# A streaming attention decode kernel: seven instead of five output blocks behind the last V quarter, the last transfer in two pieces, three more fillers, and one gather matmul per pair of heads

## The chip, the cores and the metric

One NeuronCore of one Trainium2 chip. The metric is the device time of one execution in microseconds (us). Executions are repeated, each kernel in the same rounds on the same chip as the kernel before. Two terms recur: a transfer has landed when the trace shows it finished, and the granted clock is the share of TensorE's full clock that the trace shows (1.00 is full, 0.50 half).

## The reference, cut to what matters

Four residual layers, numbered 0 to 3 here, weights A, B, A, B, one query token:

```python
# per layer: x = x + attention(layernorm(x)) @ wo
q = layernorm(x) @ wq                       # D = 640 -> 32 heads x 192
scores = einsum("bhqd,bhkd->bhqk", q, k_cache) * 192 ** -0.5   # 8192 keys a head
p = softmax(scores)
o = einsum("bhqk,bhkd->bhqd", p, v_cache)
x = x + o.reshape(1, 1, 6144) @ wo
```

All inputs are bfloat16. Every layer reads its K and V caches (about 100 MB each) once, which, with the weights, is where the 849 MB of an execution come from; a little of the first two layers is kept on the chip for the last two.

## The kernel before

Heads go in 16 pairs per layer. K and V stream into eight slots of SBUF. VectorE (DVE) multiplies K by q, TensorE (PE) sums the products with an identity matrix, softmax follows, and PE multiplies by V. A pair then has its sums on four groups of 32 partitions (a "gather" adds them up), and after every fifth pair the row of heads is turned into columns and multiplied by a block of wo.

The gather of a pair, with one FP32 matmul per head, both to PSUM partition 96:

```python
def gather(p):
    end = p == NPAIR - 1
    a, n = (slice(0, P), 1) if end else (slice(96, 97), 2)
    ...                                      # DVE: acc = sum of 8 groups of columns
    PE.wait(e, last["TO"], last["TT"])
    for h in range(2):
        if end:
            ...                              # the last pair goes to columns directly
        else:
            e = PE.op(lambda t, h=h: t.matmul(
                TB[96:97, C_O + h * DH:C_O + (h + 1) * DH], lhsT=half[:, h:h + 1], rhs=acc[:],
                start=True, stop=True), signal=h == 1, bank=TBu)
```

The order of the last transfers of layers 1 and 3, with NB wo blocks ("wob") kept back behind the last V quarter ("vq"), and the last pair's three blocks of wo ("wol") at the very end. "wol" is issued only when the columns of the first 15 pairs have been made:

```python
NB = [0, 5, 0, 5]
plan.insert(-2, ("wo", l, 2))                # 15 - NB blocks, ahead of the last pair's V
...
plan.append(("vq", l))                       # last quarter of the last pair's V
both(("wob", l))                             # NB blocks
both(("wol", l))                             # 3 blocks of the last pair
```

Filler matmuls, whose result nobody reads, stand where PE would be idle near the end: `busy(16)` ahead of the gather of pair 14, and in layer 3 `busy(6)` ahead of the wait for the last V quarter:

```python
def busy(n):
    PE.wait(ev_const, last["S"][0])
    for i in range(n):                       # identity x identity, 512 columns, to a free bank
        ...
```

## Time and profile before

| | before |
|---|---|
| median of the first three runs | 1982.81 us (1982.56 to 1983.79) |
| the same with three more runs | 1983.24 us (1982.22 to 1986.6) |
| span of the profiled run | 1980.6 us |
| DMA queue, share of 16 engines | 99.6% |
| from the landing of the last V quarter to the end | 6.4 us |

The page's lines on the busy shares, the stream and the chain stand in the prediction. To these belong the groups that the gather touches, and PE's first summing matmul of each K, L609 (line, engine, operation, out<-in, shapes, count | busy us, mean ns | idle before, releaser):

```profile
L705 PE MATMUL TB<-acc,small 128*1 128x192 f32 x240 | 81.8, 491 | 212.0 <-DVE acc L694 212.0
L716 ACT ACTIVATE rows<-TB,small 1x192 bf16<-1x192 f32 x120 | 43.2, 405 | 590.6 <-PE TB L705 590.6
L609 PE MATMUL S<-pool,ident 128*128 128x512 bf16 x128 | 62.3, 487 | 203.9 <-DVE pool L596 203.8
```

Read the first line so: 60 pairs, two heads, two records each, are 240; PE is busy with them for 81.8 us, and before them it sat idle for 212 us waiting for DVE. It is the idle time that says how little the 81.8 us are worth. In the timeline of the kernel before, one ordinary pair (start, duration, what, idle time before):

```profile
1921.64 1.44 PE L705 MATMUL TB<-acc,small 128*1 128x192 f32 x4 [3.68 <-DVE acc L694]
1923.12 0.72 ACT L716 ACTIVATE rows<-TB,small 1x192 bf16<-1x192 f32 x2 [8.01 <-PE TB L705]
1926.61 6.77 DVE L596 TENSOR_TENSOR pool<-pool,q_sb 128x3072 bf16<-128x3072 bf16 x4 [5.02 <-DMA pool<-in_B_k_cache_dram]
...
1928.43 0.61 PE L609 MATMUL S<-pool,ident 128*128 128x512 bf16 x1 [5.34 <-DVE pool L596]
```

After the gather PE is idle for another 5.34 us, until DVE has multiplied the next K; and DVE itself had waited 5.02 us for that K to land.

### The profile page before, as it was taken

What the parts mean: (1) busy time and instruction counts of PE and PEld (TensorE: products, weight loads), DVE (VectorE), ACT (ScalarE), POOL (GpSimd) and SP (SyncE); (2) the same over time, 40 slices, a digit from 0 to 9 for tenths busy, and PEclk for the clock granted to TensorE, in tenths of its full rate; (3) what the DMA queues carried; (4) which work ended last, traced back from release to release, by engine and by line L of the source; (5) the groups of instructions that cost most, each with busy time, mean ns of one, the idle gap of its engine ahead of it and who ended that gap; (6) DMA issues with size and microseconds to landing.
All of it is one profiled execution on the core that took longest, in us unless ns stands there. A gap on an engine that the chain in (4) does not pass through costs nothing.

```text
span 1980.6 us, 13743 instructions
## 1 busy us (share of the span) xinstructions
PE 1288.7 (65%) x8245; PEld 146.4 (7%) x3159; DVE 1201.3 (61%) x1376; ACT 139.9 (7%) x462; POOL 4.5 (0%) x23
## 2 busy tenths in 40 slices
PE   3567476666466666665785675666676766666658
PEld 0001001000200100100020010010002001001001
DVE  3567467467166656566745565665764775665756
ACT  0000000000000000000010000000000100000000
POOL 0000000000000000000000000000000000000000
PEclk9787776778587777777787778877886878777779
DMA  9999999999999999999999999999999999999998
GB/s 413 435 435 429 430 430 433 436 428 429 436 430 431 430 435 433 427 433 432 426 412 431 426 429 432 431 428 432 431 430 428 435 431 435 431 432 432 431 432 367
DMA packets 26786, 849.25 MB, mean 429 GB/s; under 512 B 3042, under 2 KB 3044, under 8 KB 3812
## 3 DMA queue, kind: packets, MB, share of 16 engines
q1 hardware_dynamic: 26580, 848.38, 99.6%
q8 instruction: 45, 0.74, 0.2%
q14 instruction: 17, 0.14, 0.0%
q10 hardware_dynamic: 144, 0.00, 0.0%
HBM read 848.36 MB, written 0.00 MB: 428 GB/s over the span
## 4 chain that ended last, share of the span: by engine, by line
DMA 67%; PE 19%; DVE 12%; ACT 1%; issue 0%; SPq 0%
DMA pool<-in_B_k_cache_dram 27%; DMA pool<-in_A_v_cache_dram 22%; DMA pool<-in_A_k_cache_dram 13%; DVE pool L596 10%; PE S L58 10%; DMA pool<-in_B_v_cache_dram 6%; PE OY L58 5%; PE OY L675 3%; DVE acc L694 1%; ACT p_sb L633 1%; DVE s_sb L618 1%; PE S L609 1%; PE OY L535 0%; DVE m_bf L620 0%; PE QM L623 0%
## 5 line engine op out<-in xcount | busy, mean ns | idle before, releaser
L596 DVE TENSOR_TENSOR pool<-pool,q_sb 128x3072 bf16<-128x3072 bf16 x512 | 861.1, 1753 | 235.0 <-DMA pool<-in_B_k_cache_dram 139.5
L58 PE MATMUL S<-pool,ident 128*128 128x512 bf16 x2944 | 793.4, 428 | 17.0 <-DVE pool L596 15.4
L705 PE MATMUL TB<-acc,small 128*1 128x192 f32 x240 | 81.8, 491 | 212.0 <-DVE acc L694 212.0
L58 PE MATMUL OY<-pool,p_sb 128*16 128x512 bf16 x1920 | 198.1, 488 | 0.0
L693 DVE TENSOR_SCALAR acc<-OY,small 128x192 f32<-128x192 f32 x64 | 26.7, 418 | 281.1 <-PE OY L58 251.6
L609 PE MATMUL S<-pool,ident 128*128 128x512 bf16 x128 | 62.3, 487 | 203.9 <-DVE pool L596 203.8
L675 PE MATMUL OY<-pool,p_sb 128*16 128x512 bf16 (+1 forms) x1216 | 146.3, 489 | 67.4 <-DMA pool<-in_A_v_cache_dram 59.9
L694 DVE SCALAR_TENSOR_TENSOR acc<-OY,small,acc 128x192 f32<-128x192 f32 x424 | 177.1, 418 | 14.9
L618 DVE TENSOR_REDUCE s_sb<-S 128x64 f32<-128x512 f32 x128 | 88.0, 688 | 68.0 <-PE S L58 68.0
L524 ACT ACTIVATE q_sb<-QM 128x192 bf16<-128x192 f32 x60 | 19.9, 331 | 949.8 <-PE QM L518 949.8
L716 ACT ACTIVATE rows<-TB,small 1x192 bf16<-1x192 f32 x120 | 43.2, 405 | 590.6 <-PE TB L705 590.6
L689 DVE RECIPROCAL small<-TB 1x2 f32<-1x2 f32 x64 | 11.2, 175 | 94.9 <-PE TB L648 75.2
L633 ACT ACTIVATE p_sb<-s_sb,small 64x128 bf16<-64x128 f32 x128 | 55.7, 435 | 160.8 <-DVE small L627 160.0
L609 PEld LDWEIGHTS S<-pool,ident 128*128 128x128 bf16 x128 | 12.9, 101 | 683.1 <-DVE pool L596 589.1
L648 PE MATMUL TB<-small,ones 128*1 128x2 f32 x120 | 11.4, 165 | 74.1 <-ACT p_sb L633 74.1
L675 PEld LDWEIGHTS OY<-pool,p_sb 128*16 128x16 bf16 (+1 forms) x1216 | 38.9, 106 | 213.4 <-issue 137.2
L623 PE MATMUL QM<-ident,m_bf 128*64 128x64 bf16 x128 | 14.1, 217 | 54.4 <-DVE m_bf L620 53.8
L705 PEld LDWEIGHTS TB<-acc,small 128*1 128x1 f32 x240 | 19.7, 101 | 308.1 <-DVE acc L694 280.7
L627 DVE TENSOR_REDUCE small<-QM 128x1 f32<-128x64 f32 x64 | 14.4, 225 | 35.2 <-PE QM L623 35.2
L518 PEld LDWEIGHTS QM<-rows,one_b 1*64 1x64 bf16 x120 | 6.2, 100 | 344.2 <-issue 338.4
L535 PE MATMUL OY<-oT,pool 128*128 128x1 bf16 x675 | 28.6, 178 | 1.9 <-ACT oT L581 1.9
L535 PEld LDWEIGHTS OY<-oT,pool 128*128 128x128 bf16 x675 | 27.8, 131 | 3.8 <-ACT oT L581 2.5
(74 smaller groups left out, 218.3 us busy)
## 6 DMA issues: line engine op xcount, KB each, us to landing
pool<-in_B_k_cache_dram SPq DMA_DIRECT2D x28, 6144.0 KB, 38.3
pool<-in_B_v_cache_dram SPq DMA_DIRECT2D x28, 6144.0 KB, 34.5
pool<-in_A_v_cache_dram SPq DMA_DIRECT2D x27, 6144.0 KB, 27.6
pool<-in_A_k_cache_dram SPq DMA_DIRECT2D x34, 3072.0 KB, 20.3
pool<-in_A_k_cache_dram SPq DMA_DIRECT2D x14, 6144.0 KB, 36.4
pool<-in_A_v_cache_dram SPq DMA_DIRECT2D x10, 3072.0 KB, 14.2
pool<-in_B_k_cache_dram SPq DMA_DIRECT2D x8, 3072.0 KB, 22.6
pool<-in_A_wo_dram SPq DMA_DIRECT2D x6, 2400.0 KB, 21.8
```

Of the source, the lines that this page charges most:

```text
L58: return t.add_instruction(mybir.InstMatmult(name=t.bass.get_next_instruction_name(), engine=mybir.EngineType.PE, ins=[t.lower_ap(rhs), t. ...
L524: lambda a: a.activation(q_sb[i][:], QM[:, 0:DH], ACT.Copy), e, last["q"][i], bank=QMu)
L535: e = PE.op(lambda t, i=i, c=c, f=y_first[0], fin=n[0] == "wol" and i == k - 1: t.matmul(YB[:, c:c + 1], lhsT=t3[:, i, c:D:DC], rhs=o[:, i ...
L596: e = DV.op(lambda v, d0=d0: v.tensor_tensor(k3[:, :, d0:d0 + QD], kin[:, :, d0:d0 + QD], q_sb[qi][:, d0:d0 + QD].unsqueeze(1).broadcast_t ...
L609: t.matmul(S[:, :], lhsT=ident[:], rhs=k3[:, :, d0:d0 + R], start=True, stop=fin) if d0 == 0 else
L618: lambda v, u=u: v.tensor_reduce(s[:, u * JU:(u + 1) * JU], SP_[u][:].rearrange("p (j r) -> p j r", r=R), AX.X, ALU.add), ev_S[p, u], last ...
L633: ev_p[p] = AC.op(lambda a, h=h, r=r: a.activation(p_sb[par][r, :, h], s[r, :], ACT.Exp, bias=negm[par][r, 0:1], accum_out=l_col[par][r, h ...
L675: t.matmul(o, lhsT=x, rhs=y, start=f, stop=fin) if c == 0 else
L693: v.tensor_scalar(acc[:], O[:, 0:DH], pick[:, 0:1], None, ALU.mult) if i == 0 else
L694: v.scalar_tensor_tensor(out=acc[:], in0=O[:, i * DH:(i + 1) * DH], scalar=pick[:, i:i + 1], in1=acc[:], op0=ALU.mult, op1=ALU.add)), e if ...
L705: e = PE.op(lambda t, h=h: t.matmul(TB[96:97, C_O + h * DH:C_O + (h + 1) * DH], lhsT=half[:, h:h + 1], rhs=acc[:], start=True, stop=True), ...
L716: last["TO"] = last["row_written"] = AC.op(lambda a, h=h: a.activation(orow[:, o0 + h * DH:o0 + (h + 1) * DH], TB[96:97, C_O + h * DH:C_O ...
```

## The change

Its intent: shorten what stands behind the last V quarter in layer 3, and spend less of PE on the gather. Cut to its core:

```diff
-    NB = [0, 5, 0, 5]
+    NB = [0, 5, 0, 7]
+        both_h = sb("both_h", [P, 33], F32)          # column 0: head 0, column 32: head 1, zero between
             both(("wol", l))
+            if l == 3:
+                both(("woe", l))                     # wol: two blocks, woe: the third, own semaphore
...
-                        e = PE.op(lambda t: t.matmul(TB[96:97, C_L:C_L + 2], lhsT=ones[:, 0:1], rhs=l_col[par][:],
+                        e = PE.op(lambda t: t.matmul(TB[64:97, C_L:C_L + 2], lhsT=ones[:, 0:1].broadcast_to([P, 33]), rhs=l_col[par][:],
...
+                if end and l == 3:
+                    busy(3)
                 PE.wait(e, last["TO"], last["TT"])
-                for h in range(2):
+                for h in range(2 if end else 1):
...
-                        e = PE.op(lambda t, h=h: t.matmul(
-                            TB[96:97, C_O + h * DH:C_O + (h + 1) * DH], lhsT=half[:, h:h + 1], rhs=acc[:],
-                            start=True, stop=True), signal=h == 1, bank=TBu)
+                        e = PE.op(lambda t: t.matmul(TB[64:97, C_O:C_O + DH], lhsT=both_h[:], rhs=acc[:],
+                                                     start=True, stop=True), bank=TBu)
...                                                   # ACT then reads head h from partition 64 + 32 * h
```

## The prediction

> **What bounds the kernel now.** I read the page from the top: busy shares, the 40 slices, the queues, then the chain that ended last, and then the end of the execution in the timeline, because that is where most of the diff sits.
>
> ```profile
> PE 1288.7 (65%) x8245; PEld 146.4 (7%) x3159; DVE 1201.3 (61%) x1376; ACT 139.9 (7%) x462; POOL 4.5 (0%) x23
> DMA  9999999999999999999999999999999999999998
> DMA packets 26786, 849.25 MB, mean 429 GB/s; under 512 B 3042, under 2 KB 3044, under 8 KB 3812
> q1 hardware_dynamic: 26580, 848.38, 99.6%
> DMA 67%; PE 19%; DVE 12%; ACT 1%; issue 0%; SPq 0%
> ```
>
> and the end of that chain, in order of time (start us, duration us, what):
>
> ```profile
> 1936.94 37.25 DMA pool<-in_B_v_cache_dram
> 1974.19 0.04 issue
> 1974.23 0.85 PE OY L675 x16
> ...
> 1976.04 0.89 PE TB L701 x12
> 1976.93 1.20 PE OY L567 x16
> 1978.13 0.02 issue
> 1978.15 0.43 ACT pool L760
> ```
>
> The reader is to see two things. First, no compute engine is near full (PE 65%, DVE 61%), while the one DMA queue occupies the 16 engines for 99.6% of the span. 849.25 MB at 429 GB/s is 1980 us, the whole span of 1980.6 us. An engine made faster in the middle can only help where the queue had run dry, and it hardly does. Second, the last lines are the only stretch where nothing is left to stream: the last quarter of V lands at 1974.19 us and 6.4 us of serial work follow to the end of the span. Slice 40 shows it as well: 367 GB/s against about 430 elsewhere.
>
> The end closer up, from the windows view (start:end, length, busy per engine, granted clock, DMA share, GB/s):
>
> ```profile
> 1966.00:1972.00 6.00, 4.82 (x89) 3.06 (x88) 0.17 (x1) 0.91 (x3) 0.00 (x0) 1.00 0.99 410
> 1972.00:1975.00 3.00, 2.20 (x24) 0.35 (x17) 0.00 (x0) 0.00 (x0) 0.00 (x0) 1.00 0.62 257
> 1975.00:1977.00 2.00, 1.02 (x20) 0.90 (x18) 0.84 (x2) 0.03 (x1) 0.00 (x0) 1.00 0.18 73
> ```
>
> From 1972 us some DMA engines are done and others still busy. The lagging ones set when a transfer has landed. The granted clock is 1.00 up to 1978 us, so the matmuls of the end already run at full clock.
>
> **What the Trainium skill says.** "DMA: Bandwidth & Descriptors", section "Where 436 GB/s comes from", puts a ceiling of 435 GB/s on the SBUF ports; 37 of the 40 slices here stand at 426 to 436, so the trace agrees and nothing is left to gain in the stream. The same page, "Queues, rings and completion order", says that each DMA engine consumes descriptors in ring order. The trace agrees: behind the last quarter of V stand 800 KB and 480 KB of wo (of 1024 bytes each), 1,310,720 bytes, which at 430 GB/s take 3.05 us; the 480 KB were issued at 1969.62 and took 7.6 us, so they landed at 1977.2, 3.0 us after V. "TensorE: Matmul & The Clock Gate", section "What's actually happening", has the array at half clock after an idle window of about 3.4 us. The trace agrees: a pair's four gather records take 1.44 us after an idle of 3.68 us (at 1921.64), but 0.81 us at 1965.19, where filler matmuls ran before. "FP8 and Floating Point Precision", "TensorE Precision Notes", counts 4 passes for true FP32; each head's gather shows as two records at a warm pitch of 0.162 us, which is 2 x 192 columns at 2.4 GHz, so again 4 passes.
>
> **Part 1, NB[3] from 5 to 7.** Two of the 15 row blocks of the last wo transfer move from ahead of the final V pair to behind it. 2 blocks x 128 partitions x 640 x 2 bytes = 327,680 bytes; at 430 GB/s that is 0.76 us by which the last quarter of V lands earlier: 1974.19 becomes 1973.43. Total bytes and the end of the last wo transfer stay where they were, about 1977.2. In exchange 2 blocks x 2 halves = 4 more matmuls stand after V. The 16 that now close the chain start between 1976.86 and 1977.83, a pitch of 0.065 us, so 4 cost 0.26 us. **Net -0.50 us**, if nothing else becomes the wait.
>
> **Part 2, wol split in two (two blocks, then one).** The three blocks of the last pair's wo are now two transfers of 320 and 160 KB, and only the last two matmuls wait for the second. One more issue on SP costs 0.33 us, at 1969.95, while the ring still holds megabytes: hidden. In the kernel before, the first wol weight load was at 1977.40, after the landing at 1977.2, and followed the wob matmuls without a gap, so this wait was not felt. With Part 1 the chain would reach wol at about 1976.12 + 14 x 0.065 = 1977.03, before 1977.2, and would wait; with the split the first four matmuls need only what lands 160 KB earlier (1976.8), and the last two start at about 1977.3 against a landing of 1977.2 to 1977.35. So the split protects the gain of Part 1 and adds **0 to 0.1 us** of waiting. The pieces are rows of 2560 and 1280 bytes, which I allow up to 0.1 us for.
>
> **Part 3, busy(3) before the final gather.** Three 512-column matmuls, 0.22 us each at full clock (16 of them took 3.8 us at 1960.98), plus a weight load of 0.10: 0.75 us, in the wait of 0.98 us in which PE sits while DVE sums. It fits; and as the clock was already 1.00, it wins nothing. **0**.
>
> **Part 4, the pair gather.** For 60 pairs two FP32 matmuls become one with 33 stationary columns: 240 records become 120. The cost follows the 192 moving columns, so a pair falls from 1.44 us to about 0.84 cold (0.524 + 0.32), and from 0.81 to 0.49 warm. Over the kernel PE loses some 35 us of busy time (about 58 cold pairs x 0.6) and DVE gains three tiny operations at the start, inside a 16.77 us wait for x. On the path this is worth nearly nothing: after the gather PE waits anyway for the next pair's first product on DVE (1.75 us) or for K, and the row written by ACT is needed only after five pairs. Two places could feel it. At the end of layer 3 the gather of pair 14 stands ahead of the wol issue, which would come 0.32 us earlier (1969.3); the ring is not empty then (375 to 440 GB/s to 1972), so no gain. At the end of layer 1 the queue thins after 1006 us (240 GB/s in one microsecond), but there PE waited for V at 1002.32 after the gather, which hides the saving. **0 to -0.1 us.** The sums on 33 partitions in place of one cost the same (one matmul, one reciprocal whose time barely depends on partitions: 168 to 177 ns in both forms).
>
> **Sum.** -0.50 + 0.05 + 0 - 0.05 = -0.5 us. 1982.81 - 0.5 = **1982.3 us**.
>
> **Rivals.** (a) The last wo transfer becomes the end. For it: it lands at 1977.2 whatever V does, and now there are more and smaller descriptors behind V. Against: only two matmuls (about 0.4 us with drain) stand behind it, so matmuls would end at 1977.65, and that is what Part 1 gives anyhow (1978.13 - 0.50 = 1977.63). If it lands 0.3 us late the gain shrinks to 0.2: 1982.6. (b) PE's 35 us saved are on the path somewhere. For it: the chain gives PE 19% and DVE 12%, and buffers freed sooner start transfers sooner. Against: DMA share is 99.6%, so an earlier issue only lengthens the queue; landing takes 27 to 38 us for 6 MB that need 14.6 us at 430 GB/s, so two or more transfers are always waiting. If it were so, up to 2 us: 1980.8. (c) busy(3) delays the gather: if those matmuls ran at half clock they would take 1.4 us and cost 0.4 us, cancelling the rest: 1982.7. Against: clock 1.00 in that window. (d) Nothing visible, because executions differ by more than the change: the three runs before span 1.2 us.
>
> **Range and chances.** The mechanism gives 0.2 to 0.6 us, 0.03% of the time; the spread of executions is 1.2 us in three runs, and another chip or day may add as much. I take 1981.0 to 1983.8. Two per cent would be 40 us; the whole stretch outside the stream is 6.4 us at the end and a few at the start, so faster by 2% has no place to come from, and slower by 2% would need the queue to stall, which no part of the change does. 1% and 1%.
>
> **What would show it.** In the changed kernel's trace, counted back from the end of the span: V's last quarter landing about 6.7 us before it rather than 6.4 (the end is 0.5 us earlier, the landing 0.76); wob with 14 matmuls and no wait before the last two; about 120 gather records instead of 240, PE busy down by some 35 us and GB/s unchanged near 430. Wrong would be: a DMA wait ahead of the last two matmuls longer than 0.2 us; clock under 1.00 at the final gather; V's landing not earlier against the end; or a mean rate different from 429 GB/s by over 1, which would move the time by more than all the parts.

## The result, and the profile after

| | before | after |
|---|---|---|
| median of six runs | 1983.24 us | 1982.71 us (1981.84 to 1986.04) |
| ratio | | 0.9999, 95% interval 0.9986 to 1.0011 |
| span of the profiled run | 1980.6 us | 1980.1 us |
| V's last quarter lands | 1974.19 us | 1973.31 us |
| from there to the end | 6.4 us | 6.8 us |

A ratio is the mean time of one kernel's fast runs over that of the other's of the same rounds, so it is not quite the ratio of the medians. The interval is about 5 us wide, ten times the gain that I predicted: the time alone can say that nothing large happened, and no more. What the change did is read from the traces.

The stream and the engines in the changed kernel's page, to set beside those in the prediction:

```profile
PE 1266.0 (64%) x8128; PEld 140.6 (7%) x3040; DVE 1201.7 (61%) x1379; ACT 146.1 (7%) x462; POOL 4.5 (0%) x23
DMA packets 26929, 849.24 MB, mean 429 GB/s; under 512 B 3058, under 2 KB 3188, under 8 KB 3828
q1 hardware_dynamic: 26724, 848.38, 99.7%
```

PE has 22.7 us less to do, and the stream has the same bytes at the same rate. The same groups:

```profile
L714 PE MATMUL TB<-acc,both_h 128*33 128x192 f32 x120 | 48.7, 507 | 212.3 <-DVE acc L701 212.3
L724 ACT ACTIVATE rows<-TB,small 1x192 bf16<-1x192 f32 x120 | 49.4, 412 | 565.4 <-PE TB L714 563.9
L616 PE MATMUL S<-pool,ident 128*128 128x512 bf16 x128 | 62.3, 487 | 224.0 <-DVE pool L603 224.0
```

Half the records, 33.1 us less for them. The sums on 33 partitions cost 2.7 us more (14.1 in place of 11.4 us), and ACT 6.2 us more for the same 120 operations. PE's wait for DVE before each K's first summing matmul grew from 203.8 to 224.0 us: much of what the gather gave up turned into waiting there. The end of the chain of waits (start, duration, what):

```profile
1935.94 37.37 DMA pool<-in_B_v_cache_dram
1973.31 0.04 issue
1973.35 0.85 PE OY L682 x16
...
1975.15 0.89 PE TB L710 x12
1976.05 1.53 PE OY L574 x20
1977.58 0.02 issue
1977.60 0.43 ACT pool L772
```

V lands 0.88 us earlier than in the kernel before, 20 wo matmuls in place of 16 take 1.53 in place of 1.20 us, and PE is done at 1977.58 in place of 1978.13 us, 0.55 us earlier. In this one pair of traces the working of the prediction came out nearly to the tenth. Whether that pair was typical, and which parts matter, is for the experiments.

### The profile page after: what moved, and what is told of

It is laid out like the page before. It is cut to its first block, busy times and chain, and to the rows that moved or that the text cites. A ratio compares the mean times of both kernels' runs of the same rounds, so it can differ in the third digit from the quotient of the medians.

```text
span 1980.1 us, 13511 instructions
## 1 busy us (share of the span) xinstructions
PE 1266.0 (64%) x8128; PEld 140.6 (7%) x3040; DVE 1201.7 (61%) x1379; ACT 146.1 (7%) x462; POOL 4.5 (0%) x23
## 3 DMA queue, kind: packets, MB, share of 16 engines
q1 hardware_dynamic: 26724, 848.38, 99.7%
## 4 chain that ended last, share of the span: by engine, by line
DMA 67%; PE 17%; DVE 15%; ACT 1%; issue 0%; SPq 0%
DMA pool<-in_B_k_cache_dram 27%; DMA pool<-in_A_v_cache_dram 20%; DMA pool<-in_A_k_cache_dram 14%; DVE pool L603 13%; PE S L58 7%; DMA pool<-in_B_v_cache_dram 5%; PE OY L58 5%; PE OY L682 3%; DVE acc L701 1%; ACT p_sb L640 1%; DVE s_sb L625 1%; PE S L616 0%; DVE m_bf L627 0%; PE OY L542 0%; PE QM L630 0%
## 5 line engine op out<-in xcount | busy, mean ns | idle before, releaser
L58 PE MATMUL S<-pool,ident 128*128 128x512 bf16 x2944 | 792.7, 427 | 18.0 <-DVE pool L603 16.7
L616 PE MATMUL S<-pool,ident 128*128 128x512 bf16 x128 | 62.3, 487 | 224.0 <-DVE pool L603 224.0
L58 PE MATMUL OY<-pool,p_sb 128*16 128x512 bf16 x1920 | 195.5, 493 | 0.0
L682 PE MATMUL OY<-pool,p_sb 128*16 128x512 bf16 (+1 forms) x1216 | 142.1, 491 | 66.8 <-DMA pool<-in_A_v_cache_dram 59.7
L714 PE MATMUL TB<-acc,both_h 128*33 128x192 f32 x120 | 48.7, 507 | 212.3 <-DVE acc L701 212.3
L724 ACT ACTIVATE rows<-TB,small 1x192 bf16<-1x192 f32 x120 | 49.4, 412 | 565.4 <-PE TB L714 563.9
L696 DVE RECIPROCAL small<-TB 33x2 f32<-33x2 f32 x64 | 11.1, 173 | 94.3 <-PE TB L655 77.7
L655 PE MATMUL TB<-small,ones 128*33 128x2 f32 x120 | 14.1, 187 | 74.1 <-ACT p_sb L640 74.1
L682 PEld LDWEIGHTS OY<-pool,p_sb 128*16 128x16 bf16 (+1 forms) x1216 | 34.8, 105 | 216.0 <-issue 139.1
L630 PE MATMUL QM<-ident,m_bf 128*64 128x64 bf16 x128 | 14.1, 216 | 54.4 <-DVE m_bf L627 53.9
L634 DVE TENSOR_REDUCE small<-QM 128x1 f32<-128x64 f32 x64 | 14.4, 225 | 36.6 <-PE QM L630 36.6
L714 PEld LDWEIGHTS TB<-acc,both_h 128*33 128x33 f32 x120 | 10.9, 140 | 289.6 <-DVE acc L701 284.4
## 6 DMA issues: line engine op xcount, KB each, us to landing
pool<-in_B_k_cache_dram SPq DMA_DIRECT2D x8, 3072.0 KB, 22.7
```

What stands on the lines that cost most here:

```text
L58: return t.add_instruction(mybir.InstMatmult(name=t.bass.get_next_instruction_name(), engine=mybir.EngineType.PE, ins=[t.lower_ap(rhs), t. ...
L616: t.matmul(S[:, :], lhsT=ident[:], rhs=k3[:, :, d0:d0 + R], start=True, stop=fin) if d0 == 0 else
L682: t.matmul(o, lhsT=x, rhs=y, start=f, stop=fin) if c == 0 else
L714: e = PE.op(lambda t: t.matmul(TB[64:97, C_O:C_O + DH], lhsT=both_h[:], rhs=acc[:], start=True, stop=True), bank=TBu)
L724: last["TO"] = last["row_written"] = AC.op(lambda a, h=h: a.activation(orow[:, o0 + h * DH:o0 + (h + 1) * DH], TB[64 + 32 * h:65 + 32 * h, ...
```

## The experiments

Twelve runs on three chips. The main number of each is the stretch from the landing of the last V quarter to the end of the span; it holds no streaming of K and V, so differences in how fast the stream ran do not enter it. In the diffs, "before" and "after" say which kernel was edited.

**The two kernels once more.** No edit.

> The kernel before once more: from V's landing to the end 6.4 us within 0.15; span within 4 us of 1980.6.

> The changed kernel once more, to see how far the end repeats. If the reading of the end is sound: from V's landing to the end of the span 6.8 us within 0.15, no DMA wait over 0.1 us ahead of the wo matmuls, while the whole span may differ by 1 to 4 us. If the end is itself at the mercy of the stream, it differs by 0.5 us or more.

The kernel before repeated: landing at 1974.12, end at 1980.5, 6.4 us. The changed kernel did not. V landed at 1973.74 us (issued at 1937.14, 36.6 us to landing), but the span was 1982.8 us, so 9.1 us from landing to end. The last steps of its chain hold no DMA at all:

```profile
1973.32 1.28 PE OY L682 x12
1974.60 0.54 PE S L434
1975.14 1.09 PE S L58 x5
1976.23 0.78 PE OY L682 x16
```

and the windows of that trace (start:end, length, busy of PE, PEld, DVE, ACT, POOL, granted clock, DMA share, GB/s) show what differed:

```profile
1965.00:1968.00 3.00, 1.37 (x20) 0.65 (x22) 0.74 (x2) 0.83 (x2) 0.00 (x0) 1.00 1.00 424
1968.00:1971.00 3.00, 2.75 (x43) 1.53 (x34) 0.00 (x0) 0.19 (x1) 0.00 (x0) 0.54 0.97 410
1971.00:1974.00 3.00, 2.98 (x30) 1.42 (x32) 0.17 (x1) 0.00 (x0) 0.00 (x0) 0.50 0.86 334
1974.00:1976.00 2.00, 2.00 (x10) 0.10 (x1) 0.00 (x0) 0.00 (x0) 0.00 (x0) 0.74 0.41 165
```

The clock was halved from about 1968 to 1975 us. PE fell behind, and the six fillers that stand ahead of V's last quarter (lines L434 and L58 of the chain) were still running, 1.6 us long, while V had already landed. So my expectation of 0.15 us was wrong, and neither of its two explanations held: V landed as early as in after_rounds (1973.74 us in both), where the end took 6.8 us. PE's clock made the difference, and the fillers were on the path. Their 1.6 us is not all loss: the clock came back to 1.00 while they ran, and V's last quarter then took 0.78 us.

**Part 1 alone.**

```diff
-    NB = [0, 5, 0, 5]        # before
+    NB = [0, 5, 0, 7]
```

> Part 1 alone: seven wo blocks behind the last V quarter, the last pair's wo still one transfer, no filler, old gather. My theory (the end is a race between the work after V and the last wo transfer): from the landing of the last V quarter to the end of the span about 7.0 us (6.41 in the kernel before, 6.79 in the changed one), because the six matmuls on the last pair's wo now wait 0.1 to 0.3 us for its one transfer; V lands 0.75 us earlier against the end of the stream. Rival (that transfer has landed anyway, the split is worth nothing): no wait ahead of those six matmuls and 6.7 us from V's landing to the end.

1982.61 us, span 1980.8 us. The last pair's wo, as one transfer, landed after PE was ready for it, and the chain ended with it:

```profile
1969.49 7.80 DMA rows<-in_B_wo_dram
1977.29 0.14 issue
1977.43 0.92 PE OY L567 x6
```

PE had started the first of the 14 wob matmuls at 1976.17 us; their records end at 1977.28. From V's landing (1973.5) to the end it took 7.3 us rather than the 7.0 expected; the six matmuls ran at half clock (0.92 in place of 0.57 us), which explains the difference. The rival falls: in this run the split was not worth nothing, though the wait that it removes is small: in the changed kernel the last six matmuls start 0.95 us after the first of the 14, which would have been 1977.12 here, so 0.3 us.

**Part 4 alone.** The changed kernel with the end of layer 3 put back (NB, wol, no busy(3)).

> Part 4 alone: the gather of a pair by one matmul, the end of layer 3 as before. My theory (hidden behind the stream): PE busy some 20 us below the kernel before, 429 GB/s as before, and a time within 1 us of the kernel before, inside the noise; the stretch from V's landing to the end 6.4 us as before. Rival (the gather is on the path): 10 to 30 us faster.

Four runs, 1984.48 us in the median (1983.61 to 1984.55) against 1983.14 us of the kernel before; ratio 1.0006, interval 0.9991 to 1.0021. The median is 1.3 us above, where I had expected at most 1 us. PE busy was 1265.8 us and the stream moved 429 GB/s. So the 23 us taken from PE bought nothing: my theory stands against the rival. In the profile the end was even slower, 7.5 us from landing to end, because the 16 wo matmuls took 2.25 us in place of 1.20 at a granted clock of 0.5. One profile cannot say whether the lighter gather makes that more likely.

**The gather three times over.**

```diff
-                        e = PE.op(lambda t, h=h: t.matmul(                  # before
+                        for k in range(3):
+                            e = PE.op(lambda t, h=h: t.matmul(
```

> The kernel before with every pair's gather matmuls done three times over (same result, no other change): 480 more FP32 records, some 2.9 us more of PE per pair at the low clock, 60 pairs, about 170 us of added PE work in sum. My theory (PE has that much idle time per pair while it waits for K or for DVE, and the queue of transfers hides a later release): at most 3 us slower, all of it at the ends of layers, where the gather of pair 14 stands ahead of the next transfer's issue. Rival (what the gather costs reaches the path, so that halving it must help): 50 to 170 us slower.

Four runs, 1986.3 us in the median against 1983.14, ratio 1.0019 (1.0002 to 1.0035); the whole interval lies above 1: some 3.3 us slower by the spans. The gather group grew by 136 us (81.8 to 218.2), less than the 170 I wrote: a pair took 4.00 in place of 1.44 us at half clock and 2.11 in place of 0.81 at full clock. Of that 136 us PE's wait for DVE before each K gave 80 (203.8 to 123.5). Another 43 came back with a higher granted clock (0.816 in the mean in place of 0.777; 0.809 to 0.816 in all four runs against at most 0.785 in the seven of the kernel before), probably because PE was idle less: the 2944 later matmuls that sum K took 750.1 us in place of 793.4. So 98% of the added work was hidden, and the rival of 50 to 170 us falls. My own addition, that the loss would lie at the ends of layers, was wrong for nearly all of it: V landed 3.1 us later (1977.29 us), and the end took 6.6 in place of 6.4 us, because the tripled gather of pair 14 made PE late. Most of the delay shows in the middle of layer 2. The same windows in the kernel before, then with the tripled gather:

```profile
1100.00:1200.00 100.00, 67.28 (x458) 8.60 (x192) 57.21 (x66) 6.44 (x24) 0.00 (x0) 0.78 1.00 427
1300.00:1400.00 100.00, 69.02 (x432) 8.11 (x175) 61.51 (x68) 6.28 (x22) 0.00 (x0) 0.76 1.00 430
```

```profile
1100.00:1200.00 100.00, 66.11 (x474) 11.04 (x216) 56.47 (x64) 7.10 (x26) 0.00 (x0) 0.83 0.99 420
1300.00:1400.00 100.00, 70.10 (x453) 11.08 (x199) 60.65 (x66) 6.99 (x24) 0.00 (x0) 0.80 1.00 421
```

7 and 9 GB/s less for 100 us are 0.7 and 0.9 MB, at 430 GB/s 1.6 and 2.1 us, together about what was lost. In both windows a block of wo is worked off (its matmuls run at 1174 and 1327 us in the kernel before). Layer 2 takes its K in halves of 3 MB, which need 20 us to landing, 13 us of them queueing at 430 GB/s; the whole K of 6 MB of layers 1 and 3 needs 38 us, 23 of them queueing. The queue is shorter in layer 2, so that a late release shows there is the likely reading, though no run tried it by itself. The real change went the other way by a quarter of that size, and its trace shows 429 and 432 GB/s in these windows, where a second profile of it shows 429 and 429. That is no gain that I can tell from noise.

**Nine blocks behind V.**

```diff
-    NB = [0, 5, 0, 7]        # after
+    NB = [0, 5, 0, 9]
```

> The changed kernel with nine blocks behind V in place of seven. My theory (seven is where the work after V and the wo transfer meet): V's last quarter lands another 0.75 us earlier against the end of the stream, but a wait of 0.5 to 0.8 us appears ahead of the wob matmuls, which then have 18 to do; from V's landing to the end 7.6 to 7.9 us in place of 6.8, so no gain, 0 to 0.3 us slower. Rival (V's landing alone sets the end): 7.05 us from V's landing to the end and another 0.5 us gained.

Four runs, 1983.7 us in the median against 1983.44, ratio 1.0003 (0.9986 to 1.0019). In the timeline:

```profile
1978.21 1.39 PE L574 MATMUL OY<-pool,oT 128*1 128x320 bf16 x18 [0.75 <-DMA pool<-in_B_wo_dram]
```

PE waits 0.75 us for the kept-back blocks. V landed at 1974.71 us and the end came 7.8 us later, as expected; the rival (7.05 us) falls. With five and seven blocks the end waits for V, with nine for wo, so the two meet between seven and nine; eight was not tried.

**The fillers taken out, in steps.** All from the changed kernel: without `busy(3)` (e3, one look, and again as e10 with rounds); without `busy(3)` and `busy(6)` (e6); without those and `busy(16)` in layer 3 (e9); and with more of them (e8), 18 in place of 16, 4 new ones while ACT writes pair 14's row, 8 in place of 6.

```diff
-                if end and l == 3:
-                    busy(3)             # e3, e10, e6, e9
-                        if l == 3:
-                            busy(6)     # e6, e9
```

> The changed kernel without the three filler matmuls ahead of the final gather. My theory (the clock is full there anyway): clock 1.00 up to 1977 us, the 12 records of the final gather 0.89 us as with the filler, 6.8 us from V's landing to the end. Rival (the filler keeps the clock up): those records and the 20 wo matmuls take up to twice as long, 0.9 to 1.5 us more.

> The changed kernel with neither the three filler matmuls nor the six ahead of the wait for V's last quarter. If fillers at the end matter at all, it is here: PE then has 1 to 2 us of idle before V and 1 us after it. If the clock drops, the final matmuls take up to twice as long and the stretch from V's landing to the end grows from 6.8 to 7.5 or 8.3 us; if the real work of the last 10 us is enough to hold it, nothing changes.

> The changed kernel without the three fillers ahead of the final gather, this time with rounds. Theory A: now and then half clock for the 20 wo matmuls (1 us more, as it was in two profiles without these three fillers), so 0 to 0.5 us above the changed kernel in the median. Theory B, my prediction's step (the three fillers win nothing): within 0.2 us, which these rounds can hardly resolve; the profile is to show whether clock at 1976 to 1979 us is 1.00.

> The changed kernel with no filler at all in layer 3's end (16, 6 and 3 taken out). Theory A: half clock in most of the last 15 us, PE reaches V's last quarter 1 to 3 us after it landed, and the median lies 1.5 to 4 us above the changed kernel's. Theory B: within 1 us of it.

> The changed kernel with more filler matmuls in layer 3's end: 18 in place of 16 ahead of pair 14's gather, 4 new ones while ACT writes that pair's row, 8 in place of 6 ahead of V's last quarter, 3 as before ahead of the final gather. Theory A (what the earlier profiles suggest: in some executions the granted clock halves within the last 15 us, at 1968 us in one of the changed kernel, at 1977 us in the old-end kernel with the new gather, and that costs 1 to 2.5 us, more than the whole change wins): the clock stays at 1.00 to 1978 us in the profile, V's landing to the end 6.8 us, and the median lies 0.3 to 1 us below the changed kernel's, with fewer slow outliers. Theory B (the spread comes from the stream, not from the end): same median within 0.3 us.

> The changed kernel itself in the same rounds, as the one to compare with: 1982 to 1984 us. In the profile either full clock and 6.8 us from V's landing to the end, or, as once before, half clock from 1968 us and 8 to 9 us from V's landing to the end.

e3 and e10 are the same kernel, without the three fillers. Its 20 wo matmuls took 1.52 us in e3 and 2.83 us in e10. In e3 the clock was 1.00 to the end, and landing to end took 6.7 us. In e10 it was halved from 1976.54 us to the last matmul, and the stretch took 8.05 us. By e3 alone I would have called the three fillers useless. All profiles together, by whether `busy(3)` was there:

| profile | busy(3) | wo matmuls after V, us | landing to end, us |
|---|---|---|---|
| before, before_again | no | 16 in 1.20, 1.20 | 6.4, 6.4 |
| e3 | no | 20 in 1.52 | 6.7 |
| gather x3 | no | 16 in 1.20 | 6.6 |
| e1 | no | 14 full, 6 at half clock, 0.92 | 7.3 |
| e2 | no | 16 in 2.25 | 7.5 |
| e6 | no | 20 in 2.53 | 7.8 |
| e10 | no | 20 in 2.83 | 8.05 |
| e9, no fillers | no | 20 in 1.47, half clock 1966 to 1976 | 8.3 |
| after, after_rounds | yes | 20 in 1.53, 1.54 | 6.8, 6.8 |
| e8, more fillers | yes | 20 in 1.54 | 6.8 |
| e5 | yes | 24 in 1.81 | 7.8 (the wait for wo) |
| after_again | yes | 20 in 1.47, half clock 1968 to 1975 | 9.1 |

With the three fillers the wo matmuls ran at full clock in five profiles of five; without them, and leaving out e9, in four of eight. If the fillers made no difference, four halved profiles of thirteen would still all miss these five about one time in ten, so the count alone does not show it.

The clock records of the traces say more. In all 14 traces every complete stretch at one clock lasts a whole multiple of 3.41 us, so the clock changes only on a grid of moments 3.41 us apart, and the grid lies differently in each execution. The changed kernel (clock halved at 1979.93 us, after its last matmul) and e10 chanced to have a moment at the same place (start:end, length, busy, granted clock, DMA share, GB/s; the changed kernel first):

```profile
1973.11:1976.52 3.41, 2.94 (x39) 1.54 (x39) 0.84 (x2) 0.27 (x1) 0.00 (x0) 1.00 0.41 163
1976.52:1979.93 3.41, 1.04 (x16) 0.47 (x12) 0.00 (x0) 0.43 (x1) 0.00 (x0) 1.00 0.01 2
```

```profile
1973.13:1976.54 3.41, 1.92 (x30) 1.10 (x28) 0.84 (x2) 0.00 (x0) 0.00 (x0) 1.00 0.42 173
1976.54:1979.95 3.41, 2.86 (x21) 1.14 (x20) 0.00 (x0) 0.70 (x2) 0.00 (x0) 0.50 0.04 15
```

With the fillers PE had been busy for 2.94 us before that moment and kept its clock (e8 likewise, 3.00 us at 1976.57); without them it had been busy for 1.92 us and lost it. Busy time alone does not decide it everywhere: about 1.8 us before a moment was enough in e3 at 1967.19 us and not in after_again at 1968.21. The kernel before had its moment at 1978.42 us, and its clock halved there, 0.3 us after its last matmul. That its profile shows 1.00 to the last matmul was thus in part luck.

So the fillers can be worth 0.35 to 1.3 us in an execution whose moment falls badly. How often that is stays open, and the times do not confirm a gain: in the same rounds the changed kernel had 1982.96 us in the median (1981.98 to 1984.92), without `busy(3)` 1982.59 (1981.91 to 1985.53), with no filler 1983.03 (1981.9 to 1984.64), and with more fillers 1982.56 (1982.07 to 1983.59), against 1983.51 of the kernel before; all four ratios lie between 0.9994 and 0.9997 with intervals of about 0.0025. Theory A, that the end decides the spread, is right for the profiled runs (the tripled gather left out, V landed between 1973.3 and 1974.7 us, and the rest took 6.4 to 9.1 us), and its forecast of 1.5 to 4 us for no fillers at all is not: the median did not move. One reason can be read from the profiles of e9 and after_again. When PE is late, a filler is itself on the path. With no fillers PE finished V's last quarter at 1976.3 us, with them in after_again at 1977.0 us, both at half clock before. So, as far as these single profiles show, fillers keep a full clock in some executions and seem to cost time in others. The version with more fillers is the lowest of all by median, by 0.4 us below the changed kernel as theory A said, and has the narrowest range, but no verdict sets it apart from either kernel.

## Why the prediction was right

The predicted 1982.3 us and the measured 1982.71 us differ by less than two runs of one kernel do. The closeness of the number is luck: its base of 1982.81 us became 1983.24 with three more runs, a shift nearly as large as the gain, and "no gain" on the old base would have been nearer. In both sets of rounds the changed kernel's median is 0.5 us lower (1982.71 against 1983.24, 1982.96 against 1983.51), but with intervals ten times as wide this is not shown. The prediction's rival (d), nothing visible in the time, is what came. By its steps:

- **The bound.** The stream: 99.6% and 99.7% of the engines' time, 429 GB/s before and after. Right.
- **Part 1.** V 0.76 us earlier: 0.88 in the profiled pair, 0.4 to 0.9 over all pairs of the two kernels. Four matmuls for 0.26: 0.33. Net -0.50: -0.55 in the end of PE's work. Nine blocks showed that the trade is exhausted before nine.
- **Part 2.** "0 to 0.1 us of waiting", and that the split protects the gain: without it the chain ended in the last transfer, as e1 showed; with it, in three profiles of the changed kernel, PE did not wait for it.
- **Part 3, the step that was wrong in its reason.** The prediction said of busy(3) that "as the clock was already 1.00, it wins nothing". That it costs nothing was right: PE's idle time before the final gather fell from 0.98 to 0.23 us and the gather started no later. (Its 3.8 us for 16 fillers adds two groups that overlap; from 1960.98 to 1964.60 they took 3.62.) But one trace cannot show that a clock is safe. In four of eight profiles without these fillers some or all of the last matmuls ran at half clock, which cost 0.35 to 1.3 us, and in the kernel before the clock fell 0.3 us after them. The term was 0 and should probably have been a gain with a chance attached; its mean is not shown.
- **Part 4.** Nearly all sizes held: 1.44 to 0.85 us at half clock (predicted 0.84), 0.81 to 0.51 at full clock (0.49), 33 us less in the group (35). PE's whole busy time fell by 22.7 us, not by the 35 named as a sign; the groups overlap in time, so their savings do not simply add up. The sums on 33 partitions, said to cost the same, took 187 in place of 165 ns. In the changed kernel's timeline:

```profile
1923.36 0.85 PE L714 MATMUL TB<-acc,both_h 128*33 128x192 f32 x2 [3.69 <-DVE acc L701]
1924.25 0.85 ACT L724 ACTIVATE rows<-TB,small 1x192 bf16<-1x192 f32 x2 [9.11 <-PE TB L714]
```

  Not foreseen was ACT, with 0.85 in place of 0.72 us for the two heads. At the end of layer 3, where pair 14's gather stands ahead of the last transfers, PE saves 0.30 us and ACT takes 0.13 back: from the gather's start to their issue 4.25 in place of 4.43 us, 0.18 rather than 0.32 earlier. As predicted, it makes no difference there. The rival (b), PE on the path, was refuted by the gather alone and by its tripling.
- **The range.** The spread named as 1.2 us was 4.4 and 4.2 us over six runs of the two kernels. The median lies inside the range of 1981.0 to 1983.8, two of the changed kernel's six runs above it. Two runs, 1986.6 before and 1986.04 after, lie outside what any profile here explains; their cause stays open.

## What to carry to other kernels

When a stream is 99% of the time, count only what happens after its last byte, and shift work there until the last computation and the last transfer meet; here nine blocks in place of seven gained nothing. An added-cost run (the same operation three times) is the quickest way to find out whether an operation is on the path at all, and where. A clock that read 1.00 in one trace is one sample: look at several profiles before calling a filler useless or useful, and remember that a filler delays real work whenever the engine is late.

## What the Trainium skill lacked or had wrong

- "TensorE: Matmul & The Clock Gate", section "HAM oscillation — how this bites in real kernels", gives the rule of no PE idle gaps over about 3.4 us. That rule is not enough here: in after_again the clock was halved from 1968.2 us though the gaps of the last 6 us before it were 0.59 and 1.04 us; in e10 it was halved at 1976.54 us after gaps of 0.51 and 0.98 us. The page's next section, "A second HAM failure mode: psum-queue depth-cycling", does say that frequent short idles can make the clock oscillate, but not how much idle is too much. Gaps of 0.59 and 1.03 us at the same place in the first profile of the changed kernel left the clock at 1.00.
- The same page has no word on fillers and what they cost when the engine is late: 1.6 us on the path in after_again.
- "ScalarE: Activation LUTs", section "What ACT_TABLE_LOAD costs", has back-to-back ACTIVATEs overlap by about 93 ns. With both heads read from partition 96 they do here (two of 405 ns in 0.72 us); read from partitions 64 and 96 they don't (two of 412 ns in 0.85 us). The page names no such condition; that the partitions are the cause was not tried by itself.
